# First x block from ScalarE's queue, doubled weight rows in one transfer, warm tile from VectorE, new ranks

## The chip, the cores and the metric

One core of one Trainium2 chip. The metric is the device time of one execution in microseconds, as the median of several runs.

## The reference

```python
# x: (1, 2048, 448) bf16; wqkv: (448, 1344); wo: (448, 448)
# w_in: (448, 1792); w_sp: (2048, 2048); b_sp: (2048); w_out: (896, 448)
def _A_ref(x, wqkv, wo):                       # 16 heads of 28
    W, dil = (8, 2)
    q, k, v = ...                              # from x @ wqkv
    idx = pos[:, None] - off[None, :]          # off = 0, 2, ..., 14
    kg, vg = k and v at idx                    # masked where idx < 0
    attn = softmax(einsum('bhsd,bhswd->bhsw', q, kg) * Dh ** -0.5)
    o = einsum('bhsw,bhswd->bhsd', attn, vg)
    return o (heads joined) @ wo

def _B_ref(x, w_in, w_sp, b_sp, w_out):
    z = gelu(x @ w_in)                         # 1792 columns
    z1, z2 = z[..., :896], layernorm(z[..., 896:])
    g = einsum('ts,bsf->btf', w_sp, z2) + b_sp[None, :, None]
    return (z1 * g) @ w_out

h = x + _A_ref(layernorm(x), wqkv, wo)
out = h + _B_ref(layernorm(h), w_in, w_sp, b_sp, w_out)
```

## The kernel before

**Blocks.** Tokens lie in 16 blocks of 128 (`x_tm`). Each block is normalised (statistics on VectorE, the power on POOL, the scaling on VectorE into `xn`), then transposed into `xhT`. Blocks 0 to 3 are transposed by TensorE (`xT0` to `xT3`: products with `ident` into one PSUM bank, evacuated by `xe0` to `xe3`); blocks 4 to 15 by DMA transposes from SP. The contraction dimension of 448 is cut into three chunks of 128 rows and one of 64. The 64 rows are kept twice, in partitions 0 to 63 and 64 to 127, so that two products that need them run side by side on the two halves of TensorE's rows.

**Weights.** `load_c` loads a weight in three transfers: 384 rows into chunks 0 to 2 (`wq`, `wv`, `wo`), and the last 64 rows once into each half of chunk 3 (`wq_0` and `wq_1`, and so on). q's and k's weights land in `wraw`; eight copies `wp*` on VectorE and ScalarE (line 576) put the heads at a pitch of 32 into `wqk`. They depend on all three transfers. Then come the products `qk<t>_<g>` (line 565) over six token ranges `QT`, evacuated by `qe<t>_<g>` into `qkT`; `values` (`v<b>`, line 565), evacuated into `V`; `lg` (line 842), the exponential into `E` (line 851), a mask, `o` (line 866), its DMA transpose, and `project` (`y`) with the second norm and its transposes `hT`. The second half is `z2`, `z1`, the large product `g` (line 1004) and the output product (line 1028).

**Order.** A planner (`Planner.order`) places every job once, when the program is built. It keeps a modelled time for each engine; on each engine it takes, among jobs that are not later than `LOOK` allows, the one with the lowest rank in `PRIO` (one number per job, in the order in which the jobs are made). The engines then run their own lists in that order, with semaphore waits. `ON` names the jobs of `move` that run on another engine than the default one. All plain loads are jobs of SP's queue, as are the DMA transposes. `FIRST` is the order in which the first loads are made; their ranks set the order in which SP issues them: x1, x0, `wq`, `wq_1`, `wq_0`, x2 (two blocks), x4 (four), `wv_1`, x8 (four), `wv_0`, `wv`, `wo_0`, `wo_1`, x12 (four), `wo`.

**Start.** POOL sets the tile `warm` to one and builds `ident`. A filler job on TensorE (line 1043) multiplies the two where TensorE would idle, until the modelled time `WARMT`; up to `COLD` the planner takes twice its duration. A small exponential (`tbl`, line 663) loads ScalarE's table.

The lines that the steps of the prediction touch: L591 is a plain load, L590 a DMA transpose, L576 a copy or evacuation, L565 a product in full or half tiles, L677 and L679 statistics, L688 the scaling of a norm, L716 and L719 TensorE's transposes, L1043 the filler.

Of the kernel before, what the change touches and what calls it, by code (L numbers as in the profile page):

```python
# [5 lines left out]
S_TOK = 2048  # L6
D = 448
# [5 lines left out]
NB = 16  # L13
# [11 lines left out]
LOOK = {'pe': 0.06465927487231404, 'act': 0.07391855863952959, 'dve': 0.1969035871511503, 'pool': 0.02318129821447599,  # L25
        'sp': 0.10267676699206288}
PRIO = [1, 2, 4, 3, 0, 5, 10, 9, 7, 6, 8, 13, 33, 11, 12, 34, 47, 40, 41, 45, 18, 15, 71, 0, 0, 17, 13, 12, 13, 24, 14,
# [40 lines left out]
ON = {'xe1': 'dve', 'nd0_4': 'pool', 'nd0_5': 'pool', 'nd0_7': 'pool', 'nd0_8': 'pool', 'nd0_10': 'dve', 'nd0_12':  # L68
      'dve', 'nd0_13': 'pool', 'nd0_14': 'dve', 'nd0_15': 'pool', 'wp0_0': 'act', 'wp0_1': 'dve', 'wp2_0': 'act', 'wp2_1':
      'act', 'wp3_0': 'act', 'wp3_1': 'dve', 'qe1_2': 'act', 'qe2_1': 'dve', 'qe2_3': 'act', 'qe3_1': 'act', 'qe3_3': 'dve',  # L70
      'qe4_0': 'dve', 'qe4_1': 'dve', 'qe4_2': 'act', 'qe4_3': 'dve', 'qe5_0': 'dve', 'qe5_3': 'act', 'od0': 'pool', 'od1':
      'pool', 'od2': 'dve', 'nd1_0': 'dve', 'nd1_1': 'dve', 'od3': 'dve', 've4': 'act', 'od4': 'dve', 'nd1_3': 'pool', 'od5':
      'dve', 'od6': 'pool', 'nd1_4': 'pool', 'nd1_5': 'pool', 've8': 'act', 'od8': 'pool', 'nd1_6': 'dve', 'nd1_7': 'pool',
      'od9': 'pool', 've10': 'act', 'od10': 'pool', 'od11': 'dve', 'nd1_8': 'pool', 'nd1_9': 'pool', 'od12': 'pool', 'oc12':
      'act', 'nd1_10': 'pool', 'nd1_11': 'pool', 'od14': 'dve', 'oc14': 'act', 'od15': 'pool', 'nd1_12': 'pool', 'nd1_13':
      'pool', 've16': 'dve', 'oc17': 'act', 'nd1_14': 'dve', 'nd1_15': 'dve', 'z2c1': 'act', 'z2c7': 'dve', 'z2c13': 'dve'}
RAW2 = [0, 1, 2, 1, 1, 1, 1, 2, 1, 2, 1, 0, 0, 1, 0, 0]
WLH = [4, 4, 8, 9, 18, 1, 4, 12, 24, 4, 14, 34, 6, 22, 21, 26]
GRES = 1
WARMT = 9.0  # L80
COLD = 7.2
# [123 lines left out]
class Planner:  # L205
# [9 lines left out]
    def job(self, name, eng, key, ops, dur, lat=None, acq=None, rel=None, use=(), after=(), reserve=0, tbl=None, srv=None, kind="F", peer=None):  # L215
# [3 lines left out]
        j.acq, j.rel, j.reserve, j.tbl, j.srv, j.kind = acq, rel, reserve, tbl, srv, kind  # L219
# [55 lines left out]
    def order(self):  # L275
# [37 lines left out]
        while left:  # L313
# [47 lines left out]
            if j.rel is not None:  # L361
                for b in range(j.rel.b, j.rel.b + j.rel.n):
                    free[b] = True
                    freed_at[b] = j.end + lat + FILL
# [27 lines left out]
def bass_sequential_preLN__sliding_local_dilated__mixer_gmlp__prompt_kernel(  # L392
# [14 lines left out]
    X = A_x[0]  # L407
    OUT = out[0]

    with contextlib.ExitStack() as top:  # L410
# [62 lines left out]
        negh = sb("negh", [128, 1], F32)  # L473
        rcp = sb("rcp", [128, 4, NHEAD], F32)
# [23 lines left out]
        r_xh = [spot("xh%d" % m, o_xh, 4 * S_TOK * 2) for m in range(NB)]  # L498
# [88 lines left out]
        def load(name, dst, src, writes, dur, srv, key=None, transpose=False, reads=(), after=()):  # L587
            def f(e):
                if transpose:
                    return e.dma_start(dst(), src(), transpose=True)  # L590
                return e.dma_start(dst(), src())  # L591
            nload[0] += 1
            return pl.job(name, "sp", nload[0] * 0.001 - 50 if key is None else key,
                          [(f, list(reads), list(writes), True)], dur, 0.0, after=after, srv=srv)
# [136 lines left out]
        def xh_res(lo, hi):  # L731
            return r_xh[lo // 128:(hi - 1) // 128 + 1]
# [368 lines left out]
```

## Time and profile before

| | |
|---|---|
| median of 3 runs | 243.53 us (243.46 to 243.73) |
| the profiled execution's own time | 244.28 us |
| its span, first to last instruction | 242.5 us |
| TensorE busy | 234.5 us (97%), 1735 products |
| VectorE, ScalarE, POOL busy | 153.5, 92.3, 40.0 us |
| first filler, first product on `wqk`, first on `wv` | 2.43, 8.78, 14.28 us |
| landing of x1, issue to landing | 0.79 to 2.9 us |

The profile is one execution. Times in it count from the span's start. PE is TensorE, PEld its weight loads, DVE is VectorE, ACT is ScalarE, SP is SyncE and SPq its sequencer, which issues the DMAs. "x3" behind a row is the number of instructions merged into it. The profiled execution takes 0.75 us more than the median of the unprofiled runs.

### The profile page before, as it was taken

How to read it: one execution, taken by the hardware profiler on the slowest of the kernel's cores; microseconds unless marked ns; L12 is line 12 of the kernel's file. 1: busy time of each engine (PE TensorE's matmuls, PEld its weight loads, DVE VectorE, ACT ScalarE, POOL GpSimd, SP SyncE). 2: the span in 40 equal slices, each digit the busy share in tenths (PEclk: the TensorE clock that was granted, in tenths of full speed). 3: DMA queues.
4: the chain of work that ended last, by engine and by line, in shares of the span. 5: the costliest groups of instructions: out<-in, count | busy, mean ns of one | idle time of the engine just before them, and what ended most of it. 6: DMA issues, size and time to landing. Idle time of an engine off the chain costs nothing.

```text
span 242.5 us, 4316 instructions
## 1 busy us (share of the span) xinstructions
PE 234.5 (97%) x1735; PEld 114.1 (47%) x1755; DVE 153.5 (63%) x328; ACT 92.3 (38%) x114; POOL 40.0 (16%) x96
## 2 busy tenths in 40 slices
PE   5799999999999999999999999999999999999995
PEld 3565445454545444434444444444444454444453
DVE  4799988999889899999753302602305194416263
ACT  2698768747796998963341000000000000011000
POOL 8346210123232402343111000000000000000000
PEclk9999999999999999999999999999999999999999
DMA  6945565697557878694699950000000002011002
GB/s 186 323 122 103 97 119 120 147 143 178 111 110 105 151 111 171 150 173 118 127 191 167 194 103 0 3 0 0 0 3 1 0 0 78 19 38 38 19 21 95
DMA packets 66468, 23.23 MB, mean 96 GB/s; under 512 B 58896, under 2 KB 66192, under 8 KB 66448
## 3 DMA queue, kind: packets, MB, share of 16 engines
q1 hardware_dynamic: 66448, 22.95, 45.5%
q8 instruction: 14, 0.23, 0.4%
q14 instruction: 6, 0.05, 0.1%
HBM read 6.83 MB, written 1.84 MB: 36 GB/s over the span
## 4 chain that ended last, share of the span: by engine, by line
PE 93%; DMA 2%; DVE 2%; issue 1%; SPq 1%; DVEq 0%
PE psum L1004 40%; PE psum L565 38%; PE psum L1028 9%; PE psum L866 3%; PE psum L842 3%; DMA wraw<-in_A_wqkv_dram 2%; DVE st L677 1%; SPq L591 1%; DVE wqk L576 0%; PE psum L716 0%; DVE srg L1035 0%; DVE xn L688 0%; PE psum L719 0%; DVE mv L679 0%; DVEq L183 0%
## 5 line engine op out<-in xcount | busy, mean ns | idle before, releaser
L1013 DVE TENSOR_TENSOR ub<-psum,bb 128x512 bf16<-128x512 f32 x28 | 19.3, 691 | 53.1 <-PE psum L1004 52.2
L1004 PE MATMUL psum<-wsp_hi,z2p 128*128 128x512 bf16 x220 | 50.6, 379 | 0.2
L971 ACT ACTIVATE z1p<-psum 128x1024 bf16<-128x1024 f32 x14 | 14.0, 1021 | 94.1 <-PE psum L565 94.1
L851 ACT ACTIVATE E<-psum 128x896 bf16<-128x896 f32 (+2 forms) x36 | 31.8, 929 | 8.0 <-PE psum L842 8.0
L1004 PEld LDWEIGHTS psum<-wsp_hi,z2p 128*128 128x128 bf16 x224 | 21.8, 98 | 26.3 <-issue 0.4
L565 PE MATMUL psum<-xhT,wqk 128*128 128x512 bf16 (+5 forms) x186 | 27.8, 306 | 1.8 <-DVE wqk L576 1.2
L1004 PE MATMUL psum<-wsp_la,z2p 128*128 128x512 bf16 x108 | 26.1, 379 | 0.2
L1004 PE MATMUL psum<-wsp_lb,z2p 128*128 128x512 bf16 x110 | 26.0, 379 | 0.1
L565 PE MATMUL psum<-w_in,hnT 128*128 128x448 bf16 (+1 forms) x128 | 25.2, 353 | 0.0
L565 PE MATMUL psum<-hnT,w_in 128*128 128x512 bf16 (+1 forms) x108 | 23.0, 379 | 0.4 <-issue 0.3
L1028 PE MATMUL psum<-w_out,z1p 128*128 128x448 bf16 (+1 forms) x119 | 22.5, 341 | 0.0
L930 DVE BATCH_NORM_STATS2 st<-z2p 128x6 f32<-128x448 bf16 x32 | 19.2, 615 | 4.0 <-ACT z2p L926 3.5
L857 DVE TENSOR_TENSOR E<-E,maskb 128x1792 bf16<-128x1792 bf16 (+2 forms) x18 | 19.6, 1100 | 1.3 <-ACT E L851 1.2
L677 DVE BATCH_NORM_STATS2 st<-x_tm 128x6 f32<-128x448 bf16 x32 | 19.1, 609 | 1.6 <-DMA x_tm<-in_A_x_dram 1.4
L565 PEld LDWEIGHTS psum<-xhT,wqk 128*128 128x128 bf16 (+1 forms) x192 | 13.0, 96 | 12.0 <-issue 2.3
L672 POOL TENSOR_TENSOR rs<-rs,negh 128x2 f32<-128x2 f32 (+2 forms) x22 | 17.6, 801 | 1.8
L1035 DVE TENSOR_TENSOR srg<-psum,x_tm 128x448 bf16<-128x448 f32 (+1 forms) x17 | 10.0, 593 | 11.4 <-PE psum L1028 9.6
L1004 PEld LDWEIGHTS psum<-wsp_lb,z2p 128*128 128x128 bf16 x112 | 10.9, 98 | 13.3 <-issue 0.4
L1004 PEld LDWEIGHTS psum<-wsp_la,z2p 128*128 128x128 bf16 x112 | 11.0, 98 | 13.1
L1028 PEld LDWEIGHTS psum<-w_out,z1p 128*128 128x128 bf16 x119 | 11.6, 98 | 10.2
L565 PEld LDWEIGHTS psum<-w_in,hnT 128*128 128x128 bf16 (+1 forms) x128 | 9.8, 97 | 12.3 <-issue 4.2
L565 PEld LDWEIGHTS psum<-hnT,w_in 128*128 128x128 bf16 (+1 forms) x112 | 9.1, 97 | 11.9 <-issue 2.5
(58 smaller groups left out, 233.9 us busy)
## 6 DMA issues: line engine op xcount, KB each, us to landing
w_in<-in_B_w_in_dram SPq DMA_DIRECT2D x8, 224.0 KB, 3.7
out_dram<-srg SPq DMA_DIRECT2D x16, 112.0 KB, 1.7
x_tm<-in_A_x_dram SPq DMA_DIRECT2D x3, 448.0 KB, 5.9
w_out<-in_B_w_out_dram SPq DMA_DIRECT2D x1, 784.0 KB, 5.3
wraw<-in_A_wqkv_dram SPq DMA_DIRECT2D x1, 672.0 KB, 4.8
bb<-in_B_b_sp_dram SPq DMA_DIRECT2D x1, 512.0 KB, 5.5
wv<-in_A_wqkv_dram SPq DMA_DIRECT2D x1, 336.0 KB, 6.4
wo<-in_A_wo_dram SPq DMA_DIRECT2D x1, 336.0 KB, 6.0
```

What stands on the lines that cost most here:

```text
L565: ins = e.matmul(o, w, x, start=g not in seen, stop=left[g] == 0, **kw)
L672: (lambda e: e.tensor_tensor(R, A, negh[:, 0:1].to_broadcast([128, n]), ALU.pow), [rr, r_negh], r_rs[k][m:m + n])],
L677: [(lambda e: e.bn_stats(st[:, m, :], src), [rsrc], [r_st[k][m]])], dve_t(D))
L842: ins = e.matmul(psum[:, c:c + nq], qkT[p:p + DH, 2 * g + 1, k0:k0 + NK], qkT[p:p + DH, 2 * g, t0:t0 + nq], start=True, stop=True, tile_po ...
L851: return e.activation(o, i, AF.Exp, scale=SCALE)
L857: return e.tensor_tensor(a, a, maskb[:, 0:1, pad:pad + nq].to_broadcast([NK, NHEAD, nq]), ALU.mult)
L930: [(lambda e, m=m, k=k: e.bn_stats(st3[:, m, k, :], z2p[:, m, D * k:D * (k + 1)]), [r_z2[m]], [r_st[2][m]])], dve_t(D))
L971: return e.activation(o, i, AF.Gelu_apprx_tanh)
L1004: ins = e.matmul(psv(tk), z2p[:, s, 128 * fc:128 * fc + 128], w[:, 512 * (tc % 2):512 * (tc % 2) + 512], start=(s == 0), stop=(s == NB - 1))
L1013: [(lambda e, tc=tc, s=s, tk=tk: e.tensor_tensor(ub[:, s, :], psv(tk), bb[:, 512 * tc:512 * tc + 512], ALU.add), [r_bb], [r_ub[s]])], dve_ ...
L1028: ins = e.matmul(psv(tk, 0, c1 - c0), z1p[:, fc, 128 * m:128 * m + 128], w_out[:, fc, c0:c1], start=(fc == 0), stop=(fc == FC7 - 1))
L1035: [(lambda e, m=m, s=s, tk=tk, c0=c0, c1=c1: e.tensor_tensor(srg[:, s, c0:c1], psv(tk, 0, c1 - c0), x_tm[:, m, c0:c1], ALU.add), [r_x[m]], ...
```

## The change

The first x block is loaded from ScalarE's queue; the other loads stay on SP. Each weight's last 64 rows are loaded into both halves by one transfer, with a source that is broadcast over two copies. `warm` is set by VectorE instead of POOL, the filler multiplies `warm` with itself, one product per filler job instead of two. The evacuation of block 0 is cut in two halves, from two PSUM banks, on VectorE and ScalarE (`XEH`). The table's exponential writes a scratch of its own. `LOOK`, `PRIO`, `ON` and `COLD` have new values.

```diff
+LOOK = {'pe': 1e-09, 'act': 0.12110906310208006, 'dve': 0.1670667721513695, 'pool': 0.12033511783050876, 'sp':
+        0.48715483543609656}
+PRIO = [0, 1, 2, 0, 3, 7, 6, 4, 5, 10, 9, 8, 25, 41, 34, 32, 21, 43, 30, 44, 0, 0, 18, 2, 19, 5, 4, 3, 2, 21, 15, 17, 1,
...
+ON = {'xe0_0': 'dve', 'xe0_1': 'act', 'nd0_5': 'dve', 'nd0_7': 'dve', 'nd0_11': 'dve', 'nd0_13': 'dve', 'wp0_1': 'act',
+      'wp2_0': 'act', 'wp2_1': 'act', 'wp3_0': 'act', 'wp3_1': 'act', 'qe4_1': 'dve', 'qe4_3': 'dve', 'od3': 'dve', 'nd1_5':
+      'dve', 've8': 'dve', 'nd1_6': 'dve', 'od10': 'dve', 'nd1_9': 'dve', 'oc12': 'act', 'od15': 'dve', 'oc15': 'act',
+      'nd1_13': 'dve', 'oc16': 'act', 'z2c2': 'dve', 'z2c7': 'dve'}
+XEH = {0: 2}
-COLD = 7.2
+COLD = 6.4
...
-        def load(name, dst, src, writes, dur, srv, key=None, transpose=False, reads=(), after=()):
+        def load(name, dst, src, writes, dur, srv, key=None, transpose=False, reads=(), after=(), eng="sp"):
...
-            return pl.job(name, "sp", nload[0] * 0.001 - 50 if key is None else key,
+            return pl.job(name, eng, nload[0] * 0.001 - 65 if key is None else key,
...
-                 lambda: X[128 * m0:128 * m1, :].rearrange("(m p) d -> p m d", p=128), r_x[m0:m1], 0.55, (1.6, 0.3 * (m1 - m0)))
+                 lambda: X[128 * m0:128 * m1, :].rearrange("(m p) d -> p m d", p=128), r_x[m0:m1], 0.55 if m0 else 0.45,
+                 (1.6, 0.3 * (m1 - m0)), eng="sp" if m0 else "act")
...
-            js = [load(name, lambda: t[:, 0:3, 0:n], lambda: src[0:384].rearrange("(c p) n -> p c n", p=128), [rr[0]], 0.5, (1.6, srv), key=key)]
-            for i in range(2):
-                js.append(load("%s_%d" % (name, i), lambda i=i: t[64 * i:64 * i + 64, 3, 0:n], lambda: src[384:448], [rr[1 + i]], 0.6,
-                               (1.6, srv / 6.0), key=None if key is None else key + 0.01))
+            load(name, lambda: t[:, 0:3, 0:n], lambda: src[0:384].rearrange("(c p) n -> p c n", p=128), [rr[0]], 0.5, (1.6, srv), key=key)
+            load(name + "_0", lambda: t[:, 3, 0:n], lambda: src[384:448].unsqueeze(0).to_broadcast([2, 64, n]), [rr[1]], 0.6,
+                 (1.6, srv / 3.0), key=key)
...
-        pool("warm", -60, [(lambda e: e.memset(warm[:], 1.0), [], [r_warm])], 0.4)
+        pl.job("wset", "dve", -60, [(lambda e: e.memset(warm[:], 1.0), [], [r_warm])], 0.3)
...
-        pl.job("tbl", "act", -60, [(lambda e: e.activation(warm[0:1, 0:2], warm[0:1, 0:2], AF.Exp), [r_warm], [r_warm])], 0.2, tbl="exp")
+        pl.job("tbl", "act", -60, [(lambda e: e.activation(tscr[0:1, 0:2], warm[0:1, 0:2], AF.Exp), [r_warm], [r_tscr])], 0.2, tbl="exp")
...
+                    for c in range(3):
+                        oc = (o if c < 2 else o2) + 128 * c
+                        e.matmul(psum[:, oc:oc + 128], xn[:, s, 128 * c:128 * c + 128], ident[:], start=True, stop=True)
...
+                for i in range(nh):
+                    lo, hi = 4 * i // nh, 4 * (i + 1) // nh
+                    move("xe%d_%d" % (m, i), ("act", "dve")[i], key, lambda m=m, lo=lo, hi=hi: xhT[:, lo:hi, 128 * m:128 * m + 128],
+                         lambda tk=tk, i=i, lo=lo, hi=hi: psv(tk, i).rearrange("p (c t) -> p c t", c=4)[:, lo:hi], [], [r_xh[m][i]],
+                         evac_t(512 // nh), [tk], (tk, i, 1))
...
-        pl.filler = pl.job("warm", "pe", 1e6, [(lambda e: [e.matmul(psv(tkw, 0, 256), ident[:], warm[:, 0:256], start=True, stop=True)
-                                                           for _ in range(2)][-1], [r_ident, r_warm], [])], 0.22, acq=tkw)
+        pl.filler = pl.job("warm", "pe", 1e6, [(lambda e: [e.matmul(psv(tkw, 0, 256), warm[:, 256:384], warm[:, 0:256], start=True, stop=True)
+                                                           for _ in range(1)][-1], [r_warm], [])], 0.11, acq=tkw)
```

More of the change, by code (lines that the diff above doesn't have):

```diff
@@ L24 @@
 SAME = 0.0
-LOOK = {'pe': 0.06465927487231404, 'act': 0.07391855863952959, 'dve': 0.1969035871511503, 'pool': 0.02318129821447599,
-        'sp': 0.10267676699206288}
-PRIO = [1, 2, 4, 3, 0, 5, 10, 9, 7, 6, 8, 13, 33, 11, 12, 34, 47, 40, 41, 45, 18, 15, 71, 0, 0, 17, 13, 12, 13, 24, 14,
[35 rows of a table removed]
+LOOK = {'pe': 1e-09, 'act': 0.12110906310208006, 'dve': 0.1670667721513695, 'pool': 0.12033511783050876, 'sp':
+        0.48715483543609656}
+PRIO = [0, 1, 2, 0, 3, 7, 6, 4, 5, 10, 9, 8, 25, 41, 34, 32, 21, 43, 30, 44, 0, 0, 18, 2, 19, 5, 4, 3, 2, 21, 15, 17, 1,
[35 rows of a table added]
 KEY = dict(x=-10.145, xs=0.685, qk=-3.702, qkg=-1.064, v=-1.761, ve=-6.148, qe=-3.15, lg=-1.488, ex=5.497,
@@ L67 @@
 WINB = 2
[L68 to L76, printed above, removed]
+ON = {'xe0_0': 'dve', 'xe0_1': 'act', 'nd0_5': 'dve', 'nd0_7': 'dve', 'nd0_11': 'dve', 'nd0_13': 'dve', 'wp0_1': 'act',
+      'wp2_0': 'act', 'wp2_1': 'act', 'wp3_0': 'act', 'wp3_1': 'act', 'qe4_1': 'dve', 'qe4_3': 'dve', 'od3': 'dve', 'nd1_5':
+      'dve', 've8': 'dve', 'nd1_6': 'dve', 'od10': 'dve', 'nd1_9': 'dve', 'oc12': 'act', 'od15': 'dve', 'oc15': 'act',
+      'nd1_13': 'dve', 'oc16': 'act', 'z2c2': 'dve', 'z2c7': 'dve'}
 RAW2 = [0, 1, 2, 1, 1, 1, 1, 2, 1, 2, 1, 0, 0, 1, 0, 0]
+XEH = {0: 2}
 WLH = [4, 4, 8, 9, 18, 1, 4, 12, 24, 4, 14, 34, 6, 22, 21, 26]
@@ L218, in job @@
         j.lat = lat if lat is not None else {"pe": 0.2, "act": 0.25, "dve": 0.16, "pool": 0.13, "sp": 1.5}[eng]
-        j.acq, j.rel, j.reserve, j.tbl, j.srv, j.kind = acq, rel, reserve, tbl, srv, kind
+        j.acq, j.reserve, j.tbl, j.srv, j.kind = acq, reserve, tbl, srv, kind
+        j.rel = (rel, 0, rel.n) if isinstance(rel, Ticket) else rel
         j.idx = len(self.jobs)
@@ L361, in order @@
             if j.rel is not None:
-                for b in range(j.rel.b, j.rel.b + j.rel.n):
+                tk, k, n = j.rel
+                for b in range(tk.b + k, tk.b + k + n):
                     free[b] = True
@@ L473, in bass_sequential_preLN__sliding_local_dilated__mixer_gmlp__prompt_kernel @@
         negh = sb("negh", [128, 1], F32)
+        tscr = sb("tscr", [128, 2], F32)
         rcp = sb("rcp", [128, 4, NHEAD], F32)
@@ L497, in bass_sequential_preLN__sliding_local_dilated__mixer_gmlp__prompt_kernel @@
         r_x = [Res("x%d" % m) for m in range(NB)]
-        r_xh = [spot("xh%d" % m, o_xh, 4 * S_TOK * 2) for m in range(NB)]
+        r_xh = [[spot("xh%d_%d" % (m, i), o_xh, 4 * S_TOK * 2) for i in range(XEH.get(m, 1))] for m in range(NB)]
         r_qk = [[spot("qk%d_%d" % (t, g), o_qk, 8 * S_TOK * 2) for g in range(4)] for t in range(len(QT))]
@@ L597, in load_x @@
             load("x%d" % m0, lambda: x_tm[:, m0:m1, :],
-                 lambda: X[128 * m0:128 * m1, :].rearrange("(m p) d -> p m d", p=128), r_x[m0:m1], 0.55, (1.6, 0.3 * (m1 - m0)))
-        r_wp = {("v", i): spot("wv%d" % i, o_wv, 4 * D * 2) for i in range(3)}
-        r_wp.update({("q", i): spot("wraw%d" % i, o_wr, 8 * D * 2) for i in range(3)})
+                 lambda: X[128 * m0:128 * m1, :].rearrange("(m p) d -> p m d", p=128), r_x[m0:m1], 0.55 if m0 else 0.45,
+                 (1.6, 0.3 * (m1 - m0)), eng="sp" if m0 else "act")
+        r_wp = {("v", i): spot("wv%d" % i, o_wv, 4 * D * 2) for i in range(2)}
+        r_wp.update({("q", i): spot("wraw%d" % i, o_wr, 8 * D * 2) for i in range(2)})
         def load_c(name, t, src, n, rr, srv, key=None):
-            js = [load(name, lambda: t[:, 0:3, 0:n], lambda: src[0:384].rearrange("(c p) n -> p c n", p=128), [rr[0]], 0.5, (1.6, srv), key=key)]
-            for i in range(2):
-                js.append(load("%s_%d" % (name, i), lambda i=i: t[64 * i:64 * i + 64, 3, 0:n], lambda: src[384:448], [rr[1 + i]], 0.6,
-                               (1.6, srv / 6.0), key=None if key is None else key + 0.01))
-            return js
-        W_qk = [r_wp[("q", i)] for i in range(3)]
-        W_v = [r_wp[("v", i)] for i in range(3)]
-        r_wo2 = [Res("wo_%d" % i) for i in range(3)]
+            load(name, lambda: t[:, 0:3, 0:n], lambda: src[0:384].rearrange("(c p) n -> p c n", p=128), [rr[0]], 0.5, (1.6, srv), key=key)
+            load(name + "_0", lambda: t[:, 3, 0:n], lambda: src[384:448].unsqueeze(0).to_broadcast([2, 64, n]), [rr[1]], 0.6,
+                 (1.6, srv / 3.0), key=key)
+        W_qk = [r_wp[("q", i)] for i in range(2)]
+        W_v = [r_wp[("v", i)] for i in range(2)]
+        r_wo2 = [Res("wo_%d" % i) for i in range(2)]
         for what in FIRST:
@@ L660, in bass_sequential_preLN__sliding_local_dilated__mixer_gmlp__prompt_kernel @@
             pool("mask%d" % i, 1.0, [op], 0.43)
-        r_negh = Res("negh")
+        r_negh, r_tscr = Res("negh"), Res("tscr")
         pool("negh", -59.5, [(lambda e: e.memset(negh[:], -0.5), [], [r_negh])], 0.1)
-        pl.job("tbl", "act", -60, [(lambda e: e.activation(warm[0:1, 0:2], warm[0:1, 0:2], AF.Exp), [r_warm], [r_warm])], 0.2, tbl="exp")
+        pl.job("tbl", "act", -60, [(lambda e: e.activation(tscr[0:1, 0:2], warm[0:1, 0:2], AF.Exp), [r_warm], [r_tscr])], 0.2, tbl="exp")
         def ln_rstd(k, m, n, mv, key):
@@ L710, in bass_sequential_preLN__sliding_local_dilated__mixer_gmlp__prompt_kernel, with f @@
                 s = ln_norm(0, m, mv1, x_tm, r_x[m], key, False)
-                tk = Ticket(1)
-                def f(e, s=s, tk=tk):
-                    o = tk.b * 512
+                nh = XEH.get(m, 1)
+                tk = Ticket(nh)
+                def f(e, s=s, nh=nh, tk=tk):
+                    o, o2 = tk.b * 512, (tk.b + nh - 1) * 512
                     for c in range(3):
-                        e.matmul(psum[:, o + 128 * c:o + 128 * c + 128], xn[:, s, 128 * c:128 * c + 128], ident[:],
-                                 start=True, stop=True)
+                        oc = (o if c < 2 else o2) + 128 * c
+                        e.matmul(psum[:, oc:oc + 128], xn[:, s, 128 * c:128 * c + 128], ident[:], start=True, stop=True)
                     for i in range(2):
-                        ins = e.matmul(psum[64 * i:64 * i + 64, o + 384:o + 512], xn[:, s, 384:D], ident[:],
+                        ins = e.matmul(psum[64 * i:64 * i + 64, o2 + 384:o2 + 512], xn[:, s, 384:D], ident[:],
                                        start=True, stop=True, tile_position=(0, 64 * i))
@@ L722, in bass_sequential_preLN__sliding_local_dilated__mixer_gmlp__prompt_kernel @@
                 pl.job("xT%d" % m, "pe", key, [(f, [r_xn[s], r_ident], [])], 0.3, acq=tk)
-                move("xe%d" % m, "act", key, lambda m=m: xhT[:, :, 128 * m:128 * m + 128],
-                     lambda tk=tk: psv(tk).rearrange("p (c t) -> p c t", c=4), [], [r_xh[m]], evac_t(512), [tk], tk)
+                for i in range(nh):
[3 more added lines that the diff above has]
+                         evac_t(512 // nh), [tk], (tk, i, 1))
             else:
@@ L727, in bass_sequential_preLN__sliding_local_dilated__mixer_gmlp__prompt_kernel @@
                 dma_T("xT%d" % m, lambda m=m: xhT[:, :, 128 * m:128 * m + 128], lambda s=s: xn[:, s, :],
-                      [r_xn[s], r_xnd[s]], [r_xh[m]], key)
+                      [r_xn[s], r_xnd[s]], r_xh[m], key)
         def xh_res(lo, hi):
-            return r_xh[lo // 128:(hi - 1) // 128 + 1]
+            return [q for rr in r_xh[lo // 128:(hi - 1) // 128 + 1] for q in rr]
         def wap(part0, np_, c, gg):
```

70 rows, old and new, of the table PRIO are left out of this document.

## The prediction

> **What bounds the kernel now.** I read the profile's page first: TensorE is busy 234.5 us of the 242.5 us span, 97%. The chain of waits then shows where TensorE does not set the end. From 13.05 us to 239.84 us it holds nothing but TensorE and pauses of at most 0.16 us; before that it is a transfer and VectorE:
>
> ```profile
> 2.18 0.56 SPq L591
> 2.74 0.04 issue
> 2.78 5.39 DMA wraw<-in_A_wqkv_dram
> 8.17 0.03 DVEq L183
> 8.21 0.05 issue
> 8.26 0.65 DVE wqk L576 x3
> 8.90 1.68 DVE st L677 x3
> ...
> 12.62 0.39 DVE xn L688
> 13.00 0.05 issue
> 13.05 0.34 PE psum L716 x3
> ```
>
> Columns are start, length, what. The last of the three loads of q's and k's weights is issued at 2.78 and lands at 8.17; the copies into `wqk` follow, and the products with them. The timeline of TensorE shows what waits on that:
>
> ```profile
> 6.50 1.05 PE L1043 MATMUL psum<-warm,ident 128*128 128x256 bf16 x8
> 8.78 1.56 PE L565 MATMUL psum<-xhT,wqk 128*128 128x128 bf16 x24 [1.23 <-DVE wqk L576]
> 13.95 0.40 PE L842 MATMUL psum<-qkT 28*128 28x128 bf16 x16
> 14.28 1.31 PE L565 MATMUL psum<-wv,xhT 128*128 128x448 bf16 x6
> ```
>
> Real products begin at 8.78, 0.61 after the landing, with TensorE idle for 1.23 ahead of them; the values' product (`v0`) begins at 14.28. Next I asked for busy time in windows: in 8.8 to 24, 24 to 110 and 110 to 240 us TensorE is busy 15.02, 85.18 and 129.15 us, so it idles only 1.85 us in 231.2. What the change does to the landing at 8.17 therefore passes to the end nearly one to one, and the rest of the kernel has under 1.9 us of idle time to give. The windows and the list of DMA issues price the transfer:
>
> ```profile
> 4.50:5.00 0.50, 0.50 (x4) 0.15 (x1) 0.28 (x1) 0.00 (x0) 0.42 (x3) 1.00 1.04 401
> 6.00:6.50 0.50, 0.50 (x7) 0.29 (x6) 0.50 (x1) 0.00 (x0) 0.36 (x2) 1.00 1.03 217
> 8.00:8.50 0.50, 0.00 (x0) 0.00 (x0) 0.24 (x2) 0.25 (x1) 0.00 (x0) 1.00 1.10 371
> ...
> wraw<-in_A_wqkv_dram SPq DMA_DIRECT2D x1, 672.0 KB, 4.8
> wraw<-in_A_wqkv_dram SPq DMA_DIRECT2D x2, 112.0 KB, 5.0
> ```
>
> The last two columns of a window are the mean share of the 16 DMA engines and GB/s. They are all busy at 401 GB/s while rows of 896 weights (1792 bytes) move: 25.1 GB/s for one engine, 71.5 ns for one such row. At 371 GB/s, with rows of 448 (896 bytes), one takes 38.6 ns on one engine. The 384 rows land at 1.71 + 4.8 = 6.5 us, the doubled 64 rows behind them at 8.17 at the latest.
>
> **The change part by part.**
>
> **Issue order.** By the new ranks SP issues x1, `wq`, `wq_0`, x2, x4, x8, `wv_0`, `wv`, `wo_0`, `wo`, x12. One x load leaves SP and one half-row load is gone, so `wq` goes out at 1.24 instead of 1.71 and the last load of these weights at about 1.7 instead of 2.78 (issues of 0.40 to 0.59). x0 goes out on ScalarE's queue ahead of its table load (1.28), which it puts back by some 0.45; ScalarE then idles 4.32 until 6.61, so this costs nothing, and with 0.45 more behind 6.61 only if that idle time were gone.
>
> **Doubled rows in one transfer.** `wq_0` now moves 128 rows, the same bytes as the two it replaces, but its source is two copies of 64 rows with a step of zero between them: its slowest dimension is 2, where the other plain loads ahead of 16 us have 64 or 128 partitions there. No row of the trace shows such a load, so I bound it. If its rows spread over 16 engines, each moves 8, in 8 x 71.5 ns = 0.57 us, as now. If each copy stays on one engine, two engines move 64 each, in 64 x 71.5 ns = 4.58 us, and 14 stand by. Between these ends I take the second. The copy is the only outer step that source and destination can be cut at alike, since no single step walks the source through 128 rows, and every plain load of the trace has a slowest dimension that divides into sixteen.
>
> The Trainium skill, page "DMA: Bandwidth & Descriptors", section "Rules for kernel authors", speaks against this change: a leading zero-stride broadcast of c copies confines a DMA to at most c engines. By that rule the sum is the one with two engines; the same section also advises one 128-partition transfer instead of two halves, by which it would be the one with sixteen. No run here shows either yet.
>
> With two engines: the 384 rows land at 6.5 - 0.47 = 6.0, and `wq_0` between 6.0 + 4.58 = 10.6, if its two engines are the last on these rows, and 9.8, if they are the first (the three loads now spread by 0.8, 4.6 to 5.4 us from issue to landing). I take 10.2 against 8.17: **+2.0**. With sixteen the landing moves by between 0.47 (the first issue's gain) and 1.07 (the last issue's, 2.78 to 1.71), so -0.8 in the middle.
>
> **The values' weights.** The same two engines then carry their share of x2, x4 and x8 (16 + 32 + 32 rows, 80 x 38.6 ns = 3.1), `wv_0` (64 rows, 2.5) and their share of `wv` (24 rows, 0.9): `wv` lands at 10.2 + 6.5 = 16.7. TensorE reaches `v0` at 14.28 + 2.0 = 16.3 and waits up to 0.4, unless the ranks, which put the product `qk2_3F` (26) ahead of `v0F` (38), give it work: **+0.2**. Behind `wv_0`, the row for `wo` (2.5 + 0.9) and x12 (32 rows, 1.2) hold these engines until 21.3; the DMA transposes that start at 15.90 now, and land 2.5 us after their issue, queue behind them. Their cover: TensorE first needs them for the products at 23.75, 25.9 after the shift, 4.6 behind 21.3. If that cover were gone, it would be another 1 to 2 us.
>
> **x's own path.** x1 and x0 now go out together, and `xe0`, in halves on two engines, takes 0.38 (ScalarE's 256 columns) instead of 0.60. It ends at 7.21 now, 1 us ahead of the weights. With two engines this gives nothing; with sixteen it is next in line, at 7.2.
>
> **Warm tile.** The memset goes from POOL to VectorE and the fill-in products no longer need `ident`: they start near 1.5 instead of 2.43. No real product can start before the weights, so: nothing. But with weights at 10.2 TensorE is idle from about 7.5 to 10.8, 3.3 us. At the end of the run the granted clock falls only in 244.3 to 244.6 us (0.56 in that window, 1.00 before), 4.5 us after the last product. So I count nothing, and for the upper end: TensorE's first 12 fill-in products took 2.72 us where 8 later ones took 1.05 (227 and 131 ns), over some 3 us, so up to 1.5 us if the clock falls.
>
> The Trainium skill, "TensorE: Matmul & The Clock Gate", "Part 1: The HAM clock gate", drops the clock to half after one idle window of about 3.4 us, from which the idle time here would be on the edge; the 4.5 us of this trace are longer.
>
> **Ranks and engines.** Four of six `qkT` evacuations go from VectorE to ScalarE (3 of 1.03 and one of 0.61: 3.7 us more, where it is busy 67.6 of 86 us), three copies of `otm` to POOL; all beside TensorE. The products are the same ones. The new order can win at most the 1.85 idle and some changes of tile shape (pitches of 0.15 where 0.056 is usual, so 0.09 each), or lose as much: 0, with +-0.6.
>
> **Sum:** +2.0 + 0.2 = +2.2. Against the profiled execution: span 242.5 to 244.7, its time 244.28 to 246.5. The median of the runs, 243.53, is 0.75 below the profiled time: 243.53 + 2.2 = **245.7 us**.
>
> **The rivals.**
>
> *Sixteen engines carry the doubled row.* This ends on the other side. The weights land at 7.4, products start at about 8.0, and the gain of 0.8 lasts: 242.7 (242.0 to 243.0). For it: the 64-row loads of now do fill the engines. Against it: their slowest dimension is 64. It decides at about four engines: counted from 6.0, 8.17 is kept if no engine has over (8.17 - 6.0) / 0.0715 = 30 rows, and with four each has 32. Chance 0.20.
>
> *The clock falls in the wait.* The two engines as forecast, and the products behind 10.8 run at half clock for some 3 us: 247.2. Against it: the 4.5 us above. With it I put the case that the transposes lose their cover, at the same price. Chance 0.15.
>
> *The ranks win it back.* The two engines delay the weights, but the lower values above (9.8, no wait at `v0`) and the best of the new order leave no more than 0.5: 243.0 to 244.0. Chance 0.07.
>
> **How the numbers follow.** Forecast 0.58, its own range 244.4 to 246.6. To leave out no more than 2 in 10, the range goes down into the first rival, to 242.6, and up to the second, 247.3. A measurement of this kernel can tell about 0.2%, 0.5 us, from no change. Slower by more: 0.58 + 0.15 and 0.02 of the third rival, 0.75. Same: 0.05, the rest of the third. Faster: 0.20, the first.
>
> **What would show it.** In the changed profile: the `wraw` load of 224 KB takes over 8 us from issue to landing, where 5 says sixteen engines; between 6 and 10 us the DMA share is low, with 14 engines waiting at their places; the first product on `wqk` starts near 10.8, the first on `wv` near 16.5; behind 24 us TensorE idles under 2 us as before. I am wrong if the first product on `wqk` starts before 8.8, or if it starts late and idle time behind it shrinks by as much; and the fall of the clock would show as 256-column or 128-column products at twice their pitch behind 10.8.

## The result, and the profile after

The changed kernel takes 247.31 us (246.88 to 248.14, 6 runs) beside 243.83 for the kernel before on the same chip: 1.0145 of it, 95% interval 1.0123 to 1.0167, so 3.5 us slower. The profiled execution took 248.14 with a span of 246.4 us, 3.9 over the span before.

In the rows of the changed kernel L590 is a plain load, L589 a DMA transpose, L575 a copy or evacuation, L564 a product in full or half tiles, L716 and L718 TensorE's transposes, L844 `lg` and L1045 the filler.

The chain of waits of the changed kernel (start, length, what) begins with one transfer, as before, but a longer one:

```profile
1.70 9.12 DMA wraw<-in_A_wqkv_dram
10.82 0.03 issue
10.85 0.02 DVEq L179
10.87 0.05 issue
10.92 0.47 DVE wqk L575 x2
11.39 0.05 issue
11.44 2.65 PE psum L564 x24
14.09 0.21 PE psum L1045
14.30 3.79 PE psum L564 x40
18.10 0.17 PE psum L716 x3
```

The merged row goes out 1.08 us earlier than the last of the three loads did, at 1.70, and lands 2.65 later, at 10.82. TensorE's timeline shows the start of the products, and of `v0` at 14.28 before:

```profile
11.44 2.65 PE L564 MATMUL psum<-xhT,wqk 128*128 128x128 bf16 x24 [3.10 <-DVE wqk L575]
19.15 1.31 PE L564 MATMUL psum<-wv,xhT 128*128 128x448 bf16 x6
```

The first product on `wqk` is 2.66 late and `v0` is 4.87 late: a further 2.2 us goes between them. The windows say where (us; busy time of PE, PEld, DVE, ACT, POOL; granted clock, DMA share, GB/s):

```profile
7.20:10.60 3.40, 1.14 (x11) 0.62 (x9) 0.00 (x0) 0.00 (x0) 0.77 (x3) 1.00 0.50 150
10.60:14.00 3.40, 2.56 (x25) 2.17 (x26) 3.08 (x10) 2.72 (x6) 0.05 (x1) 0.50 0.47 136
14.00:17.40 3.40, 3.40 (x34) 2.74 (x34) 3.37 (x11) 2.28 (x7) 2.23 (x4) 0.50 0.58 165
17.50:20.00 2.50, 2.50 (x41) 1.61 (x38) 2.40 (x11) 2.25 (x5) 0.71 (x2) 1.00 0.73 208
...
9.00:10.00 1.00, 0.00 (x0) 0.00 (x0) 0.00 (x0) 0.00 (x0) 0.00 (x0) 1.00 0.13 48
```

From 10.6 to 17.4 the granted clock is 0.50: the products on `wqk` of the first two blocks run slower, the first 24 in 2.65 us where the kernel before took 1.56. The profiled execution is the longest of the six, with a mean clock of 0.986 over its span. Two of the six have 0.986 and four have 0.993, which is half as long at half clock, so the median holds less of this loss than the profile. And between 9 and 10 us the DMA engines are busy for 0.13 of their time, two of sixteen, and move 48 GB/s, 24 for each of the two. SP's timeline shows what that does to the loads behind:

```profile
2.44 3.18 SPq L590 DMA_DIRECT2D x_tm<-in_A_x_dram  x3
5.67 5.70 SPq L590 DMA_DIRECT2D wv<-in_A_wqkv_dram  x2
11.41 3.45 SPq L590 DMA_DIRECT2D wo<-in_A_wo_dram  x2
14.90 0.86 SPq L590 DMA_DIRECT2D x_tm<-in_A_x_dram  x1
```

Two issues that took 0.5 to 0.7 each before now hold SP for 5.70 together. The last x load goes out at 14.90 instead of 8.36, and VectorE waits 1.48 for it at 21.58.

Behind `v0` the changed kernel is the better one in these two profiles: from the start of `v0` to the end of the last product 224.63 us (19.15 to 243.78), where before took 225.56 (14.28 to 239.84). In 24 to 240 us TensorE is busy for all 216.00, and was for 214.33 (with 0.16 of the rest behind the last product of the kernel before).

### The profile page after: what moved, and what is told of

Same layout as the page of the kernel before. It is cut to its first block, busy times and chain, and to the rows that moved or that the text cites. A ratio compares the mean times of both kernels' runs of the same rounds, so it can differ in the third digit from the quotient of the medians.

```text
span 246.4 us, 4340 instructions
## 1 busy us (share of the span) xinstructions
PE 239.2 (97%) x1760; PEld 117.1 (48%) x1760; DVE 151.0 (61%) x321; ACT 96.2 (39%) x120; POOL 41.3 (17%) x98
## 4 chain that ended last, share of the span: by engine, by line
PE 94%; DMA 4%; DVE 0%; SPq 0%; issue 0%; DVEq 0%
PE psum L564 40%; PE psum L1006 39%; PE psum L1030 9%; DMA wraw<-in_A_wqkv_dram 4%; PE psum L868 3%; PE psum L844 3%; SPq L590 0%; DVE wqk L575 0%; PE psum L716 0%; DVE srg L1037 0%; PE psum L718 0%; PE psum L1045 0%; DVEq L179 0%
## 5 line engine op out<-in xcount | busy, mean ns | idle before, releaser
L564 PE MATMUL psum<-xhT,wqk 128*128 128x512 bf16 (+5 forms) x192 | 31.3, 334 | 3.1 <-DVE wqk L575 3.1
L564 PE MATMUL psum<-w_in,hnT 128*128 128x448 bf16 (+1 forms) x128 | 24.6, 353 | 0.0
L564 PE MATMUL psum<-hnT,w_in 128*128 128x512 bf16 (+1 forms) x112 | 23.6, 380 | 0.0
L564 PEld LDWEIGHTS psum<-xhT,wqk 128*128 128x128 bf16 (+1 forms) x192 | 14.7, 108 | 14.6 <-DVE wqk L575 3.4
L675 DVE BATCH_NORM_STATS2 st<-x_tm 128x6 f32<-128x448 bf16 x32 | 18.5, 612 | 3.2 <-DMA x_tm<-in_A_x_dram 3.0
L670 POOL TENSOR_TENSOR rs<-rs,negh 128x2 f32<-128x2 f32 (+2 forms) x22 | 18.1, 822 | 1.8
L575 ACT ACTIVATE qkT<-psum 128x1024 bf16<-128x1024 f32 (+2 forms) x22 | 15.2, 714 | 5.5 <-PE psum L564 5.2
L1006 PEld LDWEIGHTS psum<-wsp_la,z2p 128*128 128x128 bf16 x112 | 11.0, 98 | 13.1
L669 POOL TENSOR_SCALAR rs<-mv 128x2 f32<-128x2 f32 (+2 forms) x22 | 7.7, 351 | 47.2 <-DVE mv L677 30.2
```

The source lines that it names most:

```text
L564: ins = e.matmul(o, w, x, start=g not in seen, stop=left[g] == 0, **kw)
L575: j = pl.job(name, eng, key, [(lambda e: e.activation(o(), i(), AF.Copy) if eng == "act" else e.tensor_copy(o(), i()), list(reads), list(w ...
L670: (lambda e: e.tensor_tensor(R, A, negh[:, 0:1].to_broadcast([128, n]), ALU.pow), [rr, r_negh], r_rs[k][m:m + n])],
L675: [(lambda e: e.bn_stats(st[:, m, :], src), [rsrc], [r_st[k][m]])], dve_t(D))
L1006: ins = e.matmul(psv(tk), z2p[:, s, 128 * fc:128 * fc + 128], w[:, 512 * (tc % 2):512 * (tc % 2) + 512], start=(s == 0), stop=(s == NB - 1))
```

## The experiments

All kernels below are the changed kernel with the edit shown, except `before_q_merged`. Times are medians, ratios are to the kernel before on the same chip.

**1. The doubled row back in two transfers (`rows16`).**

```diff
-            load(name + "_0", lambda: t[:, 3, 0:n], lambda: src[384:448].unsqueeze(0).to_broadcast([2, 64, n]), [rr[1]], 0.6, ...)
+            pl.job(name + "_0", "sp", ..., [(lambda e, i=i: e.dma_start(t[64 * i:64 * i + 64, 3, 0:n], src[384:448]),
+                                             [], [rr[1 + i]], True) for i in range(2)], 0.6, ...)
```

> The changed kernel, but each doubled row is two transfers of 64 rows again, issued one behind the other at the same place in the order. Theory (two engines carry a merged row, and TensorE's clock falls in the wait): the weights land near 7.3, the first product on wqk starts near 8.0, the granted clock stays 1.0, and the time is 242.1: 0.8 below before from the start, 0.9 from the new order behind it (from v0 to the last product 224.6 us in the changed profile, 225.6 in the one before). Rival (the new ranks and the evacuations moved to ScalarE cost the time): it stays above 243.8.

Measured: 242.13 us, 0.9931 (0.9914 to 0.9948), with 243.63 for the kernel before on that chip. The order on every engine is that of the changed kernel. The copies into `wqk` start at 7.10, products at 7.78, `v0` at 13.12, and `v0` to the end of the last product again takes 224.63 (to 237.75). The ranks and the moved evacuations are not the cost; all of it, and more, is the merged transfer.

**2. Only q's and k's row merged, in the kernel before (`before_q_merged`).**

```diff
+            if name == "wq":      # in load_c of the kernel before; one issue, none in place of wq_1
+                load("wq_0", lambda: t[:, 3, 0:n], lambda: src[384:448].unsqueeze(0).to_broadcast([2, 64, n]), ...)
```

> The kernel before with one edit: q's and k's doubled row in one broadcast transfer; order, ranks, queues and all else as before. Theory: the landing moves from 8.2 to about 11.1, the first product on wqk to 11.7, the clock falls in the wait, and the time is 247.5 to 249. Rival (the ranks cost the time, not the transfer): 243.8 as before.

Measured: 249.91, 1.0250 (1.0228 to 1.0272), a little over what was expected. The row is issued at 2.18 and lands at 12.00, the first product starts at 12.62, `v0` at 20.45. The clock fell here too: its mean over the span is 0.986. One transfer makes the old kernel 2.5% slower.

**3. What makes the transfer slow: the number of its slowest dimension, or the zero step?** These three keep the two transfers of `rows16` and read the source's rows in another order, so that its slowest dimension is 2, 4 or 8 and no step is zero. They leave the last 64 rows in another order, so they time the transfer and do not compute the layer.

```diff
-            e.dma_start(t[64 * i:64 * i + 64, 3, 0:n], src[384:448])
+            e.dma_start(t[64 * i:64 * i + 64, 3, 0:n], src[384:448].rearrange("(a b) n -> b a n", b=2))   # 4, 8
```

> rows16 with the source of each 64-row transfer read in another order of its rows, so that its slowest dimension is 2 (32 rows each, step two rows) and no step is zero; the weights' last 64 rows are permuted, which changes the result and not the work. If the slowest dimension decides how many engines carry a transfer: 32 rows of each transfer on the same two engines, 64 in all, landing near 10.8 as with the broadcast. If the zero step of the broadcast decides: as rows16, landing near 7.1.

> As two_of_64, but with the rows read so that the slowest dimension is 4 (16 rows each); the last 64 rows are permuted here too. If the slowest dimension sets the number of engines: four engines carry 16 rows of each of the two transfers, 32 in all, in half the time of two_of_64 (5.7 us from the landing of the 384 rows at 6.0 to 11.7), so the landing is near 8.8 and the first product on wqk near 9.4: slower than before's 8.8, about the point from which the prediction put the sign. If two is a special case: as rows16, 7.1.

> The same with a slowest dimension of 8 (8 rows each): eight engines, 16 rows in all, landing near 7.4 and the first product on wqk near 8.0, so faster than before.

The chain of waits of `two_of_64`, then of `four_of_16`, then of `eight_of_8`, each with the last transfer of these weights:

```profile
2.46 9.21 DMA wraw<-in_A_wqkv_dram
```

```profile
2.50 7.17 DMA wraw<-in_A_wqkv_dram
```

```profile
2.56 5.31 DMA wraw<-in_A_wqkv_dram
```

| slowest dimension | rows per engine, if it is the number of engines | landing | first product | time |
|---|---|---|---|---|
| 2 | 64 | 11.67 | 12.32 | 247.85 (one run) |
| 4 | 32 | 9.67 | 10.33 | 247.08 (one run) |
| 8 | 16 | 7.87 | 8.62 | 242.96 (one run) |
| 64 (`rows16`) | 8 | about 7.0 | 7.78 | 242.13 |

The zero step is not needed: a dimension of 2 without it lands as late as the broadcast. The kept traces also count the engines. The semaphore of a plain load in 128 partitions gets 16 landing updates, spread over the landing. For the last transfer of these weights one update comes within 1.1 us of the issue, and behind it, up to the landing, come two in the changed kernel and in `two_of_64`, four in `four_of_16` and eight in `eight_of_8`; in `rows16` all 16 come between 6.12 and 6.99, the landing. So the number of engines is the slowest dimension in these runs, up to 16. The price of a row is not one number: the landing moves by 2.00 from 64 rows to 32 (62 ns for each row of 1792 bytes) and by 1.80 from 32 to 16 (112 ns), because other loads run on the same engines; in 6.2 to 9.6 us of `four_of_16` the DMA share is 1.00 (the row stands in the last section). The time of `four_of_16` also holds a fall of the clock, and its four engines are not its only loss. In `two_of_64` the DMA share while it waits is again that of two engines:

```profile
10.00:11.00 1.00, 0.00 (x0) 0.00 (x0) 0.00 (x0) 0.00 (x0) 0.00 (x0) 1.00 0.13 49
```

**4. The clock (`keep_warm`, `q_merged`, `q_merged_warm`).** `keep_warm` adds fill-in products where TensorE waits:

```diff
+            if hot and j.eng == "pe" and j.name.startswith("qk"):     # once, ahead of the first product on wqk
+                sch.issue("pe", lambda e, ...: [e.matmul(psum[:, o:o + 256], warm[:, 256:384], warm[:, 0:256], ...)
+                                                for _ in range(26)][-1], [r_warm], list(brs))
```

> The changed kernel with 26 more fill-in products (2.8 us) ahead of the first product on wqk, so that TensorE does not idle while it waits. Theory: the landing stays at 10.8 and the first product at 11.4, the granted clock stays at 1.0, and the 6.5 us from there to the next transpose on TensorE shrink to about 4.3 as before: 245.1. Rival (these 6.5 us are set by the five copies on ScalarE, not by the clock): no change, 247.3.

Half right, and the time is a miss: 247.50, 1.0144 (1.0124 to 1.0165), no faster. Its profiled execution (247.05) is 1.1 us shorter than that of the changed kernel, which was one of the two with the longer loss of clock; the medians do not differ. In its timeline of TensorE the clock's part is gone, 5.70 us from the first product to `v0` instead of 7.71:

```profile
11.57 1.56 PE L564 MATMUL psum<-xhT,wqk 128*128 128x128 bf16 x24 [0.77 <-DVE wqk L575]
17.27 1.31 PE L564 MATMUL psum<-wv,xhT 128*128 128x448 bf16 x6
26.61 0.56 PE L868 MATMUL psum<-V,E 128*128 128x29 bf16 x16 [0.24 <-DVE E L859]
28.93 0.37 PE L844 MATMUL psum<-qkT 28*128 28x112 bf16 x8 [0.16 <-DVE otm L879]
```

The last two rows are new waits of TensorE, for VectorE, and `v0` to the last product takes 225.44 (17.27 to 242.71) instead of 224.63. VectorE's list is in order: a norm statistic of x12, which lands at 21.70 here, stands in it ahead of the masks and of `otm`. In the changed kernel TensorE was too late itself to meet this. So I took the narrow transfers for `wv` and `wo` away and left q's and k's:

```diff
-            if True:
+            if name != "wq":      # two transfers of 64 rows for wv and wo, the merged one for q and k
```

> The changed kernel with the merged transfer for q's and k's weights alone; wv and wo are two transfers of 64 rows each. Nothing narrow stands ahead of x12 but the one row. Theory A (the late weights and the fallen clock are the cost): landing near 10.8, clock fallen, and 247.0 to 248.1, within 0.4 of the changed kernel. Theory B (the late x12 behind the narrow wv and wo, for which VectorE waits, carries over 1 us of it by itself): 246.3 or less.

> The same with the 26 fill-in products ahead of the first product on wqk. Theory A and B (clock and late x12 are two chains side by side, and either alone keeps the loss): with both gone only the late landing is left, the first product on wqk at 11.5 and v0 at 17.3, 4.1 behind rows16 and constant from there on: 246.3. If the clock costs nothing: as q_merged. If x12 was not what took 0.8 us back in keep_warm between 25 and 36 us: 247.1 or more.

Without the fill-in products 248.62, 1.0204 (1.0183 to 1.0224); with them 246.36, 1.0109 (1.0089 to 1.0129), as expected. The first product on `wqk` and `v0`, without and then with them:

```profile
12.24 2.65 PE L564 MATMUL psum<-xhT,wqk 128*128 128x128 bf16 x24 [3.99 <-DVE wqk L575]
19.51 1.31 PE L564 MATMUL psum<-wv,xhT 128*128 128x448 bf16 x6
```

```profile
12.15 1.56 PE L564 MATMUL psum<-xhT,wqk 128*128 128x128 bf16 x24 [0.87 <-DVE wqk L575]
17.64 1.31 PE L564 MATMUL psum<-wv,xhT 128*128 128x448 bf16 x6
```

The clock alone is worth the difference, 2.3 us between the medians and 1.87 between the two `v0`. From `v0` both take 224.62 to the end of the last product. TensorE no longer waits for VectorE there, which bears out what `keep_warm` ran into. The price of that wait is less sure: `keep_warm` lies 0.35% or 0.85 us over `q_merged_warm`, with intervals that overlap, and in the two profiles it loses 0.82 behind `v0` but starts `v0` 0.37 earlier.

`q_merged` was expected within 0.4 of the changed kernel and is 1.3 over it. In its profile the row lands at 11.62, 0.8 later than in the changed kernel, because one of its two engines finished 0.8 behind the other. All its timed runs have a mean clock of 0.986, where four of the changed kernel's six have 0.993. Why one engine lags was not tried.

**5. Narrow rows for `wv` and `wo` only (`q_rows16`).** The condition above turned round.

> The changed kernel with two transfers of 64 rows for q's and k's weights alone; wv and wo keep the merged transfer on two engines. Theory: only the transfer that TensorE waits for costs; wv lands near 12.4, ahead of v0 at about 13.5, so the time is that of rows16 within 0.5. Rival (every narrow transfer delays what stands behind it on its two engines, the DMA transposes too): at least 1 us over rows16.

Measured: 242.67, 0.9953 (0.9935 to 0.9971), 0.5 over `rows16`: at the edge of what was expected. Nearly all of the loss is the one transfer that TensorE waits for.

**6. x0 on SP again.** `rows16_x0_sp` gives the job of x0 to SP in the planner; `x0_sp_same_order` leaves the plan as it is and only issues x0 from SP.

```diff
-                 (1.6, 0.3 * (m1 - m0)), eng="sp" if m0 else "act")
+                 (1.6, 0.3 * (m1 - m0)), eng="sp")                                              # rows16_x0_sp
-                key = sch.issue(j.eng, fn, reads, writes, dma=len(op) > 3)
+                key = sch.issue("sp" if j.name == "x0" else j.eng, fn, reads, writes, ...)     # x0_sp_same_order
```

> rows16 with x0 issued on SP again, at its rank ahead of or behind x1 (the planner may place other jobs anew). If moving x0 to ScalarE's queue is what brings the weights forward: one issue of 0.4 us later, 242.5. If one issue fewer does nothing, because all transfers share the same engines: 242.1.

> rows16 with x0 issued by SP ahead of x1, and every engine's order otherwise as in rows16 (rows16_x0_sp let the planner place all jobs anew). If its loss came from the new order and not from the queue: 242.1 to 242.6, the weights landing 0.4 later at about 7.4. If the queue matters by itself: over 244.

`rows16_x0_sp` takes 252.27, 1.0358 (1.0326 to 1.0389), far outside both expectations. Its first product starts at 8.10, 0.3 behind `rows16`; what is lost is lost later, in the new order, as its windows show:

```profile
24.00:110.00 86.00, 80.01 (x860) 39.79 (x865) 67.52 (x135) 63.80 (x74) 18.85 (x40) 1.00 0.62 115
```

TensorE idles 6 us there, where `rows16` idles none. The ranks are the same list; giving the modelled issue of 0.45 us to SP was enough to place the jobs otherwise. With the order kept, x0 on SP costs 242.87, 0.9959 (0.9942 to 0.9976), 0.3% or 0.7 us over `rows16`: the weights' copies start at 7.8 instead of 7.1. So moving x0 to ScalarE's queue is worth about that much; the two intervals overlap. In the profiles, this one of the longest of its twelve executions, `v0` comes at 13.84 here, 13.12 in `rows16` and 14.28 in the kernel before. How the other 0.44 us divide among the saved issue, the warm tile and the cut evacuation was not tried.

**7. Fewer fill-in products (`rows16_trim`).**

```diff
+            if j.name == "warm" and j.eng == "pe":     # leaves out the 23rd to the 28th
```

> rows16 without the six fill-in products that stand right ahead of the first product on wqk (7.12 to 7.78, on the chain of waits there, while the copies into wqk are ready from about 7.4). If they delay it: the first product on wqk starts near 7.45, and 241.8. If the next weight copies set the pace behind it: 242.1.

Measured: 242.05, 0.9933 (0.9912 to 0.9954), as `rows16`. The first product starts at 7.29, half a microsecond earlier, and `v0` at 13.11 as in `rows16`: the transposes of blocks 2 and 3 set it, which wait for VectorE.

## Why the prediction was right or wrong

The direction was right, and so was its main mechanism, two engines for the merged row. The size was too small, 2.2 us where 3.5 were measured, and 247.31 lies just beyond the upper end of 247.3. One term of the sum had its mechanism wrong, the clock. By its steps:

**The bound.** Right: the landing passes to the end one to one. With the same order, `v0` to the last product takes 224.6 in seven profiles, whether `v0` starts at 13.1, 17.6 or 19.2, and 225.1 to 225.6 in four others.

**Two engines.** Right. Of the two ends, 0.57 and 4.58 us, the second was it, and experiment 3 shows what sets it here: the slowest dimension is the number of engines that share the rows. The place of the sign was right as well: four engines lose (first product 10.33), eight win (8.62).

**The landing, +2.0.** Under-sized: it measured +2.65. The term was counted landing to landing with 71.5 ns for a row, and 5.3 us went between the landing of the 384 rows (1.25 + 4.3 = 5.5) and 10.82, 83 ns for each of the 64 rows. The trace's list of transfers shows where the rest went. Of rows of 1792 bytes 27 start in 9 to 10 us, when nothing else moves: 74 ns for one on each of the two engines. In 6.5 to 8.0, where x's loads keep the DMA share at 1.04, 30 start, 100 ns for one. The last row ends at 10.34 and counts as landed 0.48 later. The forecast let the two engines carry x's rows only behind the merged row, and they carried some of them beside it.

**The clock, 0.** This is the step that failed. It was a rival with a chance of 0.15, and it happened: 2.2 us in the profile, 1.9 to 2.3 between `q_merged` and `q_merged_warm`, and presumably less in the four executions of the changed kernel with 0.993. The rival's 247.2 comes so near to 247.31 in part by luck, since it holds neither the longer landing nor what the order gained. The reasoning took the 4.5 us of idle time at the end of the run for the time after which the clock falls. In the changed kernel it fell 2.3 us after the last fill-in product (8.34 to 10.6), before a wait of 3.1 was over, and it came back 6.8 us later, twice 3.4. Its changes lie on a grid of about 3.4 us, and a step in which TensorE was only partly busy was enough. The Trainium skill's page "TensorE: Matmul & The Clock Gate" has that figure, in "What's actually happening" and the table behind it (a busy or idle window of about 3.4 us), and the trace agrees with the step. Its condition for the fall, an idle window, is stricter than what was measured: the step 7.2 to 10.6 held 1.14 us of products and the clock fell. The 4.5 us at the end of the run before fit the same grid: the step of 237.48 to 240.89 us was busy for 2.35 us and left the clock up, the next one was empty, and the clock fell at its end. So the 4.5 us were one step and what was left of another, and no time of idling that a wait must reach.

**The values' weights, +0.2.** Hidden in the changed kernel, where `v0` came at 19.15, after `wv` had landed. With the clock kept up (`keep_warm`) it is there: the weight loads of `v0` wait 0.3 us for `wv`. The queue behind the narrow rows was priced about right (x12 expected at 21.3, it landed at 21.56), but its cover, which the prediction held to be 4.6 us, was thinner on another path: not the transposes but VectorE's list in order. With the clock kept up it costs 0.8 us in the profile of `keep_warm`; in the changed kernel the slow products hid it. The prediction let the two add up; they lie side by side.

**Ranks and engines, 0 +- 0.6.** On the good side, by how much is open. The two profiles have 0.93 us less behind `v0`, beyond the range. But the profiled execution of the kernel before is 0.45 to 0.75 over its medians. `rows16` lies 1.50 under the kernel before by the medians, and 1.16 of that is ahead of `v0` in the profiles, so about 0.3 is left (an estimate), inside the range.

**Sum.** +2.65, +2.2 and -0.93 make 3.9, the difference of the two profiled spans. The 3.5 between the medians hold less of the clock and less of the order; they were not taken apart. The rival of sixteen engines gave 242.7; `rows16`, which is that case, measured 242.13, 1.5 under the kernel before on its chip where 0.8 was forecast. `v0` comes 1.16 earlier there, more than the 0.8, and about 0.3 is left for the order behind it.

## What to carry to other kernels

Merging two transfers into one is no gain in itself: look at the slowest dimension of the transfer, and keep it from becoming small (8 and 64 did well here, 2 and 4 did not). Two transfers of 64 rows here beat one broadcast of 2 x 64 by 5.2 us (242.13 against 247.31). Here a wait of 3.1 us put `v0` 4.87 us late, because the clock fell in it and the slow products came on top; and when one cost has been removed and the time stays, look for a second chain beside it before calling the first one free, as `keep_warm` and `q_merged_warm` show together.

## What the runs showed of the hardware that was not expected

The granted clock changes on steps of 3.4 us, and it falls without an empty step. It fell behind a step of `four_of_16` in which TensorE was busy 1.99 of 3.40 us, and not behind one of the kernel before with 2.17 of 3.40:

```profile
6.20:9.60 3.40, 1.99 (x18) 1.06 (x16) 0.73 (x2) 0.38 (x1) 1.64 (x6) 1.00 1.00 248
9.60:13.00 3.40, 2.67 (x26) 2.22 (x27) 3.20 (x10) 2.83 (x6) 0.20 (x1) 0.50 0.79 229
13.00:16.40 3.40, 3.40 (x35) 2.77 (x33) 3.37 (x13) 2.16 (x7) 2.08 (x4) 0.50 0.66 214
```

```profile
5.40:8.80 3.40, 2.17 (x21) 1.24 (x20) 1.54 (x5) 1.15 (x3) 1.87 (x7) 1.00 1.06 305
```

The first fence is `four_of_16`, the second the kernel before. The busy time of a step, as the profile counts it, does not give the edge by itself: at the end of their runs `q_merged` and `before_q_merged` kept the clock over steps with 1.65 us (242.48 to 245.89) and 1.85 us (243.99 to 247.40). Nor is there a share that brings the clock back: 2.67 of 3.40, in the second row, did not, and in `before_q_merged` it rose at 5.08, where the fill-in products go from 227 ns each to 131, behind a step with 2.65 (1.66 to 5.08). What else counts was not tried. Where the steps lie against the start differs between the profiles (the first recorded change of the clock comes at 4.5 to 7.5 us), which would explain why one kernel has means of 0.986 and 0.993.

A transfer on two engines also holds up the queue that issues it: SP took 5.70 us for the two issues of `wv`, where `rows16`, in the same order, took 1.75 for three, and the DMA share was down to 0.13 in 9 to 10 us. And it holds back what stands behind it on its two engines: of the 16 landing updates of the load of x2, fourteen came by 6.40 us in the changed kernel and the last two at 11.36 and 11.39, behind the merged row.
